# A mixture's first product as seven block products of Strassen's scheme, with its joined weights kept in DRAM

## The chip, the cores and the metric

The kernel runs on one core of one Trainium2 chip. The metric is device time in microseconds (us), the median of several executions. The core has TensorE (PE, matmuls, which write to PSUM), VectorE (DVE), ScalarE (ACT), GpSimd (POOL) and SyncE (SP, which issues nearly all DMAs here). Each engine takes its instructions in the order in which they were recorded.

## The reference

Two parts, one after the other, in float32:

```
attention:  B=4, H=8, S=768, D=64; q and k are assigned to one of 16 clusters;
            scores between different clusters are masked; softmax; times v
x = attention output as [4, 768, 512]
h = (x^T U) V ;  u = x + h^T                    (rank 32, over the 768 positions)
ch = max(u @ w_ch1, 0) @ w_ch2                  (512 -> 2048 -> 512)
out = u + ch
```

The products `u @ w_ch1` and `max(...) @ w_ch2` are what the change works on; the text calls them the first and the second product. The weights arrive as 64-bit words, and the kernel makes float32 of them with a scaling on ACT (`upper`) and three bit operations on DVE (`join`).

## The kernel before, in words

The attention runs over 16 pairs of heads (`i` = 0 to 15, 12 steps of time each). Every function is put into a list with a time (`at(time, fn, ...)`, in units of such steps); the list is sorted by time and then run, so that the table of numbers decides the order of the instructions on every engine, and `keep_order` fixes it. `M0` is the time at which the mixture begins. The order says nothing about durations: an engine waits where its next instruction's operands are not there.

To reach float32 accuracy with the fast matmul type, every operand of the mixture is split into a high part (a cast on ACT) and a low part (a subtraction), and each product takes three matmuls: high times high, high times low, low times high.

The mixture before goes over 8 half batches of 384 rows (`i`) and 16 tiles of 128 hidden columns (`f`). `gemm1(i, f)` makes 12 matmuls (4 tiles of the 512 inputs, three each) with 384 moving columns into one PSUM bank (L629, L630, L631). ACT takes the positive part as `hh` (L634), DVE the low rest as `hl` (L635). `gemm2(i, f)` makes 9 matmuls with 512 columns (3 tiles of rows, three each) into three banks `y` (L645 to L647). `finish(i)` adds `u` (L653) and writes out. `turn_u` transposes `u` for the next half batch and splits it (L618, L620, L621).

The weights lie split in SBUF from their joining to the end, in four groups of 8 pieces of 128x512 (`load_weights`): group 0 is joined during the attention, group 1 towards its end, groups 2 and 3 in the first steps of the mixture. The low parts are subtracted by POOL, four of group 1 by DVE (L208). A piece's joining is L174, L175, L177 with a result in PSUM on the way, or L181, L183, L186 in SBUF alone. POOL otherwise adds up the softmax weights (L515). Work tiles in PSUM (`work`) are 4 banks throughout, `y` another 4.

The order on SP: loads for the attention, raw weights (`rw`), `u` to DRAM and back (`u_scr`), outputs. `rowmax_place` sends the negative row maxima of the scores through a small DMA from ACT's queue (`arena<-mT`), and the second half of each score matmul (L502) waits for it.

## Time and profile before

| what | us |
|---|---|
| median of 3 runs (lowest, highest) | 1023.95 (1021.68, 1024.12) |
| span of the profiled execution, its first to its last instruction | 1023.5 |
| PE busy | 999.9 |
| DVE, ACT, POOL busy | 488.9, 350.6, 361.8 |
| DMA, moved | 87.71 MB |

The profiled execution's own time is known as its span alone; it lies between the runs' lowest and highest. Busy PE time is counted with modelled ends of matmuls that overlap, so that distances between starts are used below where a matmul's price is needed. The mixture's first matmul starts at 468.34 us of the span. A row of the timeline gives start, duration, engine, line, operation, tile written and tiles read, count, and in brackets the idle time ahead of it and what ended it.

### The profile page before, as it was taken

What the parts mean: (1) busy time and instruction counts of PE and PEld (TensorE: products, weight loads), DVE (VectorE), ACT (ScalarE), POOL (GpSimd) and SP (SyncE); (2) the same over time, 40 slices, a digit from 0 to 9 for tenths busy, and PEclk for the clock granted to TensorE, in tenths of its full rate; (3) what the DMA queues carried; (4) which work ended last, traced back from release to release, by engine and by line L of the source; (5) the groups of instructions that cost most, each with busy time, mean ns of one, the idle gap of its engine ahead of it and who ended that gap; (6) DMA issues with size and microseconds to landing.
All of it is one profiled execution on the core that took longest, in us unless ns stands there. A gap on an engine that the chain in (4) does not pass through costs nothing.

```text
span 1023.5 us, 13820 instructions
## 1 busy us (share of the span) xinstructions
PE 999.9 (98%) x5419; PEld 796.3 (78%) x5419; DVE 488.9 (48%) x914; ACT 350.6 (34%) x573; POOL 361.8 (35%) x246
## 2 busy tenths in 40 slices
...
GB/s 164 190 132 128 145 148 104 199 156 156 108 207 139 125 109 180 58 131 107 188 111 63 1 4 59 1 62 1 1 62 1 2 61 1 62 1 1 31 1 31
DMA packets 28675, 87.71 MB, mean 86 GB/s; under 512 B 4874, under 2 KB 9476, under 8 KB 28100
## 3 DMA queue, kind: packets, MB, share of 16 engines
...
q8 instruction: 42, 0.69, 0.3%
...
## 4 chain that ended last, share of the span: by engine, by line
PE 90%; DVE 5%; ACT 1%; issue 1%; DMA 1%; POOL 1%; ACTq 0%; SPq 0%; DVEq 0%; POOLq 0%
PE o_ps L523 12%; PE ps_h L629 9%; PE ps_h L631 9%; PE ps_h L630 9%; PE y L647 9%; PE y L646 9%; PE y L645 9%; PE ps_max L462 7%; PE st L500 6%; PE st L502 6%; DVE m L464 2%; PE ps_sim L352 1%; PE ps_sum L535 1%; PE ps_uT L618 1%; PE ps_oT L556 1%
## 5 line engine op out<-in xcount | busy, mean ns | idle before, releaser
L515 POOL TENSOR_TENSOR T<-T,pr 128x768 f32<-128x768 f32 x120 | 228.1, 1901 | 48.9 <-ACT pr L505 20.5
L635 DVE SCALAR_TENSOR_TENSOR hl<-ps_h,hh 128x384 fp32r<-128x384 f32 x128 | 71.3, 557 | 360.9 <-ACT hh L634 360.9
L464 DVE TENSOR_REDUCE m<-ps_max 128x1 f32<-128x384 f32 x384 | 195.4, 547 | 85.4 <-PE ps_max L462 83.5
L634 ACT ACTIVATE hh<-ps_h 128x384 fp32r<-128x384 f32 x128 | 62.9, 492 | 381.3 <-PE ps_h L631 381.3
L505 ACT ACTIVATE pr<-st 128x768 f32<-128x768 f32 x192 | 154.8, 811 | 81.2 <-PE st L502 63.3
L523 PE MATMUL o_ps<-pr,vt 128*64 128x384 f32 x768 | 133.7, 499 | 0.0
L462 PE MATMUL ps_max<-arena 128*128 128x384 f32 x384 | 125.8, 376 | 7.7 <-ACT sims L355 2.4
L646 PE MATMUL y<-w2l,hh 128*128 128x512 f32 x288 | 113.6, 395 | 0.0
L500 PE MATMUL st<-arena 128*128 128x384 f32 x384 | 106.0, 357 | 1.8 <-ACT pr L505 1.8
L523 PEld LDWEIGHTS o_ps<-pr,vt 128*64 128x64 f32 x768 | 53.2, 139 | 68.0 <-issue 62.8
L462 PEld LDWEIGHTS ps_max<-arena 128*128 128x128 f32 x384 | 70.3, 191 | 44.5 <-issue 17.9
L502 PE MATMUL st<-arena 97*128 97x384 f32 x384 | 100.4, 343 | 2.9 <-DMA arena<-mT 2.7
L500 PEld LDWEIGHTS st<-arena 128*128 128x128 f32 x384 | 66.3, 191 | 17.7 <-issue 9.9
L515 POOL TENSOR_TENSOR T<-pr 128x768 f32<-128x768 f32 x30 | 56.4, 1881 | 60.7 <-ACT pr L505 60.7
L647 PE MATMUL y<-w2h,hl 128*128 128x512 f32 x192 | 76.1, 396 | 0.0
L647 PE MATMUL y<-arena,hl 128*128 128x512 f32 x192 | 76.0, 396 | 0.0
L645 PE MATMUL y<-w2h,hh 128*128 128x512 f32 x192 | 75.1, 391 | 0.0
L645 PE MATMUL y<-arena,hh 128*128 128x512 f32 x192 | 74.8, 390 | 0.0
L502 PEld LDWEIGHTS st<-arena 97*128 97x128 f32 x384 | 71.1, 192 | 3.9 <-issue 2.8
L646 PEld LDWEIGHTS y<-w2l,hh 128*128 128x128 f32 x288 | 54.0, 188 | 9.1
L527 ACT COPY os<-o_ps 128x384 f32<-128x384 f32 x32 | 15.3, 479 | 106.5 <-PE o_ps L523 106.5
L629 PE MATMUL ps_h<-arena,w1h 128*128 128x384 f32 x128 | 44.7, 350 | 0.2 <-DVE arena L621 0.2
...
## 6 DMA issues: line engine op xcount, KB each, us to landing
...
```

What stands on the lines that cost most here:

```text
L462: nc.tensor.matmul(ps[:, 0:HS], x1[:, 0, g // 2, g % 2, t * P:(t + 1) * P], x1[:, 1, h, g % 2, :], start=True, stop=True)
L464: nc.vector.reduce_max(live["m2", i][:, h, u:u + 1], ps[:, 0:HS], axis=AX.X)
L500: nc.tensor.matmul(st[:, j, 0:HS], x1[:, 1, hk, j, ks], x1[:, 0, h, j, :], start=True, stop=False)
L502: nc.tensor.matmul(st[:, j, 0:HS], x2[0:97, 1, hk, j, ks], x2[0:97, 0, h, j, :], start=False, stop=True)
L505: nc.scalar.activation(pr, st[:, :, 0:HS], AF.Exp, scale=SCALE)
L515: eng.tensor_add(T, live["p", i, h, 0] if c == 1 else T, live["p", i, h, c])
L523: nc.tensor.matmul(o_ps[64 * j:64 * j + 64, 0:HS], vv[:, c, j, :], pr[:, j, :], start=(c == 0), stop=(c == NT - 1))
L629: nc.tensor.matmul(ps[:, 0:HS], w1h[:, d, fs], uh[:, d, :], start=(d == 0), stop=False)
L630: nc.tensor.matmul(ps[:, 0:HS], w1h[:, d, fs], ul[:, d, :], start=False, stop=False)
L645: nc.tensor.matmul(y[t], hh[:, ts], w2h[:, f % FG, :], start=(f == 0), stop=False)
L646: nc.tensor.matmul(y[t], hh[:, ts], w2l[:, f % FG, :], start=False, stop=False)
L647: nc.tensor.matmul(y[t], hl[:, ts], w2h[:, f % FG, :], start=False, stop=(f == NF - 1))
```

## The change

The first product of a whole batch is computed by blocks. `u` transposed (512 x 768) is cut into 2 x 2 blocks `b11` to `b22` of 256 inputs by 384 rows; the weights of two tiles of hidden columns (`k` and `k + 8`) into 2 x 2 blocks `a11` to `a22` of 128 columns by 256 inputs. Four sums of the `a` (`s1` to `s4`, L653, POOL) and four of the `b` (`t1` to `t4`, L627, POOL) are made, and seven products of one `a` or `s` with one `b` or `t` (Winograd's form of Strassen's scheme) stand for eight. A product is 6 matmuls of 384 columns (L687 to L689). Where PSUM added up before, seven additions of DVE that read the product in PSUM (L697) and one copy of ACT (L701) now put the results together in SBUF tiles `c0` and `c1`; `hh` and `hl` are then made of two tiles at once, 128x768 (L730, L727), from SBUF.

A group `g` is one batch `b` with one pair `k` of tiles: 4 batches x 8 pairs = 32 groups, each 7 products and 6 `gemm2` of 6 matmuls (L740 to L742). The `gemm2` of a group stand between the products of the next. The work tiles in PSUM are 2 banks from `M0` on, `y` 6.

The joined weights are no longer kept split in SBUF. Each joined half block is written to DRAM (`w_scr`, L211), and for every group its 128x1024 block of the first and of the second weights are read back (`fetch_w`, L644), summed (L653) and split (`split_w` L660 and L662, `split_w2` L669 and L671): high parts on ACT, the low ones of the first weights on POOL in batch 0 and on DVE afterwards, those of the second weights on POOL. 16 of the 32 joinings stand in the attention, from its fourth pair of heads to its twelfth (pace 6.5), 16 in groups 1 to 5 (pace 1.985, where a group is 7). Joining in the mixture works in SBUF alone: L189, L190, L192.

`u` of batch 0 is fetched, turned and split within the last two pairs of heads, that of the next batch in groups `k` = 5 to 7: 8 turns (L620, copies on ACT L622), four sums on POOL (L627), seven splits (ACT L633, DVE L634). The many times of the attention's tables are shifted slightly.

The order at three places. First, DVE while weights are being joined in the mixture (before: half batch 0; `rv`, `xt` belong to the last pair of heads):

```order
L545 TENSOR_SCALAR rv<-ps_sumT 128x12
L547 RECIPROCAL rv<-rv 128x12
L557 TENSOR_TENSOR xt<-ps_oT,rv 128x3x128
L635 SCALAR_TENSOR_TENSOR hl<-ps_h,hh 128x384
L181 TENSOR_SCALAR rw_t<-rw_g 128x512
L186 SCALAR_TENSOR_TENSOR rw_t<-rw,rw_t 128x512
L183 SCALAR_TENSOR_TENSOR rw_t<-rw_g,rw_t 128x512
```

and now, in group 2 (`c_5406` is its `c0`):

```order
L697 TENSOR_TENSOR c_5406<-ps_h,rw_g 128x384
L189 TENSOR_SCALAR rw_b<-rw_g 128x512
L190 SCALAR_TENSOR_TENSOR rw_b<-rw_g,rw_b 128x512
L192 SCALAR_TENSOR_TENSOR rw_t<-rw,rw_b 128x512
L697 TENSOR_TENSOR rw_g<-ps_h,rw_g 128x384
L697 TENSOR_TENSOR rw_t<-ps_h,rw_g 128x384
```

Between two results of PE there was one `hl`; now the three operations of a joining stand between additions that empty PSUM. Of these joinings groups 1 to 5 hold 2, 4, 3, 4 and 3.

Second, DVE at the change of batch, before (`y_5101` is the half batch that ends):

```order
L621 TENSOR_TENSOR ul<-ps_uT,uh 128x384
L635 SCALAR_TENSOR_TENSOR hl<-ps_h,hh 128x384 x2
L653 TENSOR_TENSOR u<-y_5101,u 128x512
L653 TENSOR_TENSOR u<-y_5102,u 128x512
L653 TENSOR_TENSOR u<-y_5103,u 128x512
L635 SCALAR_TENSOR_TENSOR hl<-ps_h,hh 128x384 x11
```

and now, from group 6 into group 7 of batch 0:

```order
L634 TENSOR_TENSOR arena<-turned,arena 128x768
L697 TENSOR_TENSOR c_6142<-ps_h,rw_t 128x384
L727 SCALAR_TENSOR_TENSOR hl<-c_6142,hh 128x768
L634 TENSOR_TENSOR arena<-turned,arena 128x768 x2
L697 TENSOR_TENSOR c_6201<-ps_h,rw_g 128x384
L634 TENSOR_TENSOR arena<-turned,arena 128x768
L697 TENSOR_TENSOR rw_g<-ps_h,rw_g 128x384
L660 TENSOR_TENSOR combos_107<-rw,combos_107 128x768
```

The splitting of the next operand was four short operations per half batch that read PSUM; it is seven of 128x768 per batch that read SBUF alone, put between the additions of one group's length.

Third, PE where the last pair of heads is mixed (`mix_v`: L585 before, L578 now), before:

```order
L647 MATMUL y_5103<-arena,hl 128x512
L585 MATMUL ps_h<-x_5293,v_133 128x512 x3
L629 MATMUL ps_h<-arena 128x384
L630 MATMUL ps_h<-arena 128x384
L631 MATMUL ps_h<-arena 128x384
```

and now, behind group 0's last product:

```order
L687 MATMUL ps_h<-arena,combos_107 128x384
L688 MATMUL ps_h<-arena,combos_107 128x384
L689 MATMUL ps_h<-arena,combos_107 128x384
L578 MATMUL ps_h<-x_5187,v_145 128x512 x3
L687 MATMUL ps_h<-arena,combos_5077 128x384
L688 MATMUL ps_h<-arena,combos_5077 128x384
L689 MATMUL ps_h<-arena,combos_5077 128x384
```

Three `mix_v` had a whole tile step (12 + 9 matmuls) between them and the next three; now there is one product of 6 matmuls.

The diff, cut to what is spoken of:

```
-NG = 4
-FG = NF // NG
+NK = NF // 2
...
+PACE, LATE, EARLY = 6.5, 1.985, 16
...
+    "add_w":    (   0.2,    0.8,    1.4,      2),
+    "split_w":  (  2.12,    2.5,  4.908,    5.3),
+    "relu":     (   4.3,    4.5,    6.2,    6.4),
+    "split_w2": (   3.1,    3.5),
...
+    w_scr = [[dram.tile([P, 1024], F32, name=f"w_scr{k}_{m}") for m in range(2)] for k in range(NK)]
...
+        t = home[0].tile([P, 512], I32, name="rw_t")[0:r, 0:n]
+        b = (work("ps_t").bitcast(I32) if home[0] is raw else home[0].tile([P, 512], I32, name="rw_b"))[0:r, 0:n]
+        nc.vector.tensor_scalar(b, g, 3, None, op0=ALU.logical_shift_left)
+        nc.vector.scalar_tensor_tensor(out=b, in0=g, scalar=-0x80000000, in1=b,
+                                       op0=ALU.bitwise_and, op1=ALU.bitwise_or)
+        nc.vector.scalar_tensor_tensor(out=t, in0=low, scalar=29, in1=b,
+                                       op0=ALU.logical_shift_right, op1=ALU.bitwise_or)
+        return rw, g, t
...
+    blocks = sorted(((k, m) for k in range(NK) for m in range(2)), key=lambda x: (x[0] + x[1], -x[1]))
+
+    def load_weights(s, stage):
+
...
+            nc.sync.dma_start(out=w_scr[k][m][:, cols], in_=parts.pop(("w", s))[2].bitcast(F32))
+            stored.add((k, m, half))
...
-        hi, lo = (x[:, d, :] for x in turned[i % 2])
-        nc.scalar.copy(hi, ps[:, 0:HS])
-        nc.vector.tensor_sub(lo, ps[:, 0:HS], hi)
...
-        ps = work("ps_h")
-        for d in range(ND):
-            nc.tensor.matmul(ps[:, 0:HS], w1h[:, d, fs], uh[:, d, :], start=(d == 0), stop=False)
-            nc.tensor.matmul(ps[:, 0:HS], w1h[:, d, fs], ul[:, d, :], start=False, stop=False)
-            nc.tensor.matmul(ps[:, 0:HS], w1l[:, d, fs], uh[:, d, :], start=False, stop=(d == ND - 1))
...
+    def operand(b, o):
+
+        s = (7 * b + order.index(o)) % 9
+        at = 0 if s == 8 else 2 * XS + 2 * HB * s
+        return [arena[:, at + k * HB:at + (k + 1) * HB].rearrange("p (d q) -> p d q", d=2) for k in range(2)]
+
...
+        pool["w"] = ctx.enter_context(tc.tile_pool(name="ps_m", bufs=2, space=PSUM, side="right", reuse_waits="tile"))
+        pool["y"] = ctx.enter_context(tc.tile_pool(name="ps_y", bufs=6, space=PSUM, reuse_waits="tile"))
+        combos.append(sb.tile([P, 2, 1792], F32R, name="combos1"))
+        live["w2", 0] = sb.tile([P, 2, 2, 512], F32R, name="w2_0")
...
+    def add_u(o):
+
+        i0, i1 = {"t3": ("b22", "b12"), "t1": ("b12", "b11"), "t2": ("b22", "t1"), "t4": ("t2", "b21")}[o]
+        nc.gpsimd.tensor_sub(homes[o], homes[i0], homes[i1])
+
+    def split_u(b, o):
+
+        x = homes[o]
+        hi, lo = (m.rearrange("p d q -> p (d q)") for m in operand(b, o))
+        nc.scalar.copy(hi, x)
+        nc.vector.tensor_sub(lo, x, hi)
...
+    def fetch_w(k, m):
+
+        if m == 0:
+            t = raw.tile([P, 512], I64, name="rw").bitcast(F32)
+        else:
+            t = pool["sb"].tile([P, 1024], F32, name="w2f")
+        live["f", k % NK, m] = t
+        nc.sync.dma_start(out=t, in_=w_scr[k % NK][m])
...
+    def add_w(k, o):
+
+        x, s = live["f", k % NK, 0], sums_w
+        a21, a11, a12, a22 = (x[:, 256 * i:256 * i + 256] for i in range(4))
+        s2, s3, s1, s4 = (s[:, 256 * i:256 * i + 256] for i in range(4))
+        out, op, i0, i1 = {"s1": (s1, ALU.add, a21, a22), "s3": (s3, ALU.subtract, a11, a21),
+                           "s2": (s2, ALU.subtract, s1, a11), "s4": (s4, ALU.subtract, a12, s2)}[o]
+        nc.gpsimd.tensor_tensor(out=out, in0=i0, in1=i1, op=op)
+
+    def split_w(k, part, low):
+
+        x, cols = (live["f", k % NK, 0][:, 256:1024], slice(0, 768)) if part == 0 else (sums_w, slice(768, 1792))
+        hi, lo = (combos[k % 2][:, m, cols] for m in range(2))
+        if low:
+            (nc.gpsimd if k < NK else nc.vector).tensor_sub(lo, x, hi)
+        else:
+            nc.scalar.copy(hi, x)
+
+    def split_w2(k, low):
+
+        x = live["f", k % NK, 1]
+        hi, lo = (live["w2", k % 2][:, m].rearrange("p f n -> p (f n)") for m in range(2))
+        if low:
+            nc.gpsimd.tensor_sub(lo, x, hi)
+        else:
+            nc.scalar.copy(hi, x)
+
+    products = (("a11", "b11"), ("a12", "b21"), ("s2", "t2"), ("s3", "t3"), ("a22", "t4"), ("s1", "t1"), ("s4", "b22"))
+
...
+        b, k = divmod(g, NK)
+        a, o = products[p]
+        c0 = 256 * factors.index(a)
+        ah, al = (combos[k % 2][:, m, c0:c0 + 256].rearrange("p (d f) -> p d f", d=2) for m in range(2))
+        oh, ol = operand(b, o)
+        ps = work("ps_h")[:, 0:HS]
+        for d in range(2):
+            nc.tensor.matmul(ps, ah[:, d], oh[:, d], start=(d == 0), stop=False)
+            nc.tensor.matmul(ps, ah[:, d], ol[:, d], start=False, stop=False)
+            nc.tensor.matmul(ps, al[:, d], oh[:, d], start=False, stop=(d == 1))
+
...
+        if p == 0:
+            live["p1"] = temp("rw_g")
+            nc.scalar.copy(live["p1"], ps)
+        elif p == 1:
+            combine(half(0)[:, 0], ps, live["p1"])
+        elif p == 2:
+            live["u2"] = temp("rw_g")
+            combine(live["u2"], ps, live.pop("p1"))
+        elif p == 3:
+            live["u3"] = temp("rw_t")
+            combine(live["u3"], ps, live["u2"])
+        elif p == 4:
+            combine(half(0)[:, 1], live["u3"], ps, ALU.subtract)
+        elif p == 5:
+            u4 = temp("rw_t")
+            combine(u4, ps, live.pop("u2"))
+            live["u4"] = u4
+            combine(half(1)[:, 1], ps, live.pop("u3"))
+        else:
+            combine(half(1)[:, 0], ps, live.pop("u4"))
+
+    def gemm2(g, j):
+        b, k = divmod(g, NK)
+        if k == 0:
+            live["y", b, j] = pool["y"].tile([P, 512], F32, name=f"y_{j}", tag="y")
+        t, q = divmod(j, HT)
+        y, (hh, hl), w2 = live["y", b, j], live["h", g, t], live["w2", k % 2]
+        ts = slice(q * P, (q + 1) * P)
+        for f in range(2):
+            nc.tensor.matmul(y, hh[:, f, ts], w2[:, 0, f, :], start=(k == 0 and f == 0), stop=False)
+            nc.tensor.matmul(y, hh[:, f, ts], w2[:, 1, f, :], start=False, stop=False)
+            nc.tensor.matmul(y, hl[:, f, ts], w2[:, 0, f, :], start=False, stop=(k == NK - 1 and f == 1))
...
+    for g in range(ng):
+        b, k = divmod(g, NK)
+        m = M0 + 7 * g
+        own = mlp[("first", "second")[g]] if g < 2 else None
+        relus, w2s = (own[7:11], own[11:13]) if own else (mlp["relu"], mlp["split_w2"])
+        for p in range(7):
+            at(m + (own[p] if own else p), product, g, p)
+        for k4, step in enumerate(relus):
+            at(m + step, relu, g, k4 // 2, k4 % 2 == 1)
+        for low, step in enumerate(w2s):
+            at(m + step, split_w2, g, low == 1)
+        if g + 1 < ng:
+            weights_of(g + 1, m)
+            at(m + mlp["fetch_w"][0], fetch_w, g + 1, 1)
+        if g + 2 < ng:
+            at(m + mlp["fetch_w"][1], fetch_w, g + 2, 0)
+        for j in range(6):
+            m2 = m + (own[13 + j] if own else 7 + mlp["gemm2"][0] + mlp["gemm2"][1] * j if g + 1 < ng else 7 + 0.1 * j)
+            at(m2, gemm2, g, j)
+            if k == NK - 1:
+                at(m2 + 0.3 if g + 1 < ng else m2 + 0.05, finish, b, j)
...
+            elif k == NK - 2:
+                for h in range(2):
+                    for d in range(ND):
+                        at(m + mlp["turn_u"][0] + mlp["turn_u"][1] * (ND * h + d), turn_u, b + 1, h, d)
+                splits(m, b + 1, mlp["split"])
...
+    w1 = bits["w1"].reshape(2, 2, P, 2, NK, P).transpose(4, 0, 3, 2, 1, 5)
+    w1 = np.stack([w1[:, d, f] for f, d in ((1, 0), (0, 0), (0, 1), (1, 1))], axis=2)
+    w2 = bits["w2"].reshape(2, NK, P, DM).transpose(1, 2, 0, 3)
+    weights = np.stack([w1.reshape(NK, P, 1024), w2.reshape(NK, P, 1024)], axis=1)
```

286 lines of the change are left out of this document (145 added, 141 removed).

## The prediction

> **What bounds the kernel now.** I read the page's busy lines first, then the busy times by stretches, then PE's timeline, then the durations of single lines.
>
> ```profile
> span 1023.5 us, 13820 instructions
> PE 999.9 (98%) x5419; PEld 796.3 (78%) x5419; DVE 488.9 (48%) x914; ACT 350.6 (34%) x573; POOL 361.8 (35%) x246
> PE 90%; DVE 5%; ACT 1%; issue 1%; DMA 1%; POOL 1%; ACTq 0%; SPq 0%; DVEq 0%; POOLq 0%
> 100.00:400.00 300.00, 297.34 (x1798) 202.34 (x1799) 226.08 (x447) 169.96 (x247) 239.82 (x130) 1.00 0.55 146
> 583.00:651.40 68.40, 68.40 (x350) 61.84 (x350) 12.93 (x23) 9.79 (x20) 0.00 (x0) 1.00 0.07 24
> ```
>
> The last two rows are stretches of the attention and of the mixture (length, then busy PE, weight loads, DVE, ACT, POOL, granted clock, DMA). PE is the bound in both. In the mixture nothing else is near: of 68.4 us DVE works 12.9, ACT 9.8, POOL none. Whatever PE need not do there comes off the end, as long as the idle engines do what replaces it in time. So there are two questions: what does PE save, and where does it begin to wait.
>
> ```profile
> 702.48 0.33 PE L629 MATMUL ps_h<-uh,arena 128*128 128x384 f32 x1
> 704.41 0.34 PE L631 MATMUL ps_h<-uh,arena 128*128 128x384 f32 x1
> 704.58 0.39 PE L645 MATMUL y<-arena,hh 128*128 128x512 f32 x1
> 706.66 0.33 PE L629 MATMUL ps_h<-uh,arena 128*128 128x384 f32 x1
> ```
>
> Distances between starts are the price: 12 matmuls of the first product take 704.58 - 702.48 = 2.10 us, 0.175 each; 9 of the second 2.08, 0.231 each.
>
> **What PE saves.** The first product goes from 1536 matmuls (8 x 16 x 12) to 1344 (32 x 7 x 6), of the same 384 columns and with one weight load each; the second product's 1152 and the transposes stay. 192 x 0.175 = **33.6 us**. A group then takes PE 42 x 0.175 + 36 x 0.231 = 15.67 us. Left alone this gives 1023.5 - 33.6 = 989.9.
>
> **What the other engines get.** The nearest rows:
>
> ```profile
> L621 DVE TENSOR_TENSOR ul<-ps_uT,uh x16: 542/557/558, 524.2 to 947.0; 128x384 fp32r<-128x384 f32 x16
> L515 DVE TENSOR_TENSOR T<-T,pr x8: 945/954/2021, 58.5 to 466.9; 128x768 f32<-128x768 f32 x8
> L183 DVE SCALAR_TENSOR_TENSOR rw_t<-rw_g,rw_t x16: 691/692/1670, 470.9 to 536.1; 128x512 int32<-128x512 int32 x16
> L186 DVE SCALAR_TENSOR_TENSOR rw_t<-rw,rw_t x16: 679/687/694, 470.1 to 535.4; 128x512 int32<-128x512 int32 x16
> L181 DVE TENSOR_SCALAR rw_t<-rw_g x16: 408/418/759, 469.6 to 533.6; 128x512 int32<-128x512 int32 x16
> L515 POOL TENSOR_TENSOR T<-T,pr x120: 1804/1846/2493, 40.6 to 468.0; 128x768 f32<-128x768 f32 x120
> L208 POOL TENSOR_TENSOR w2l<-rw_t,arena x4: 1283/1294/1298, 488.8 to 502.2; 128x512 fp32r<-128x512 f32 x4
> L505 ACT ACTIVATE pr<-st x192: 789/812/832, 35.2 to 462.7; 128x768 f32<-128x768 f32 x192
> ```
>
> (Minimum, median, maximum in ns.) A DVE addition that reads a product in PSUM: 0.56 us. DVE on two SBUF operands: 0.95 for 768, 0.69 for 512, so on that line 1.21 for 1024. POOL: 1.85 for 768, 1.29 for 512, so 2.40 for 1024 and 0.74 for 256. A joining on DVE: 0.42 + 0.69 + 0.69 = 1.80.
>
> A late group (batches 1 to 3): DVE 7 x 0.56 + 2 x 0.95 (`hl`) + 0.95 + 1.21 (low weights) = 8.0 us; POOL 4 x 0.74 + 2.40 = 5.4; ACT, at 0.8 to 1.1 for each of six operations, under 6. All fit into 15.67. Two PSUM banks mean that a product's bank must be read before the product after next. Between them lies mostly a product and two `gemm2` steps (1.05 + 2 x 1.39 = 3.8 us), behind the first and the seventh product 2.4. The tightest is the seventh's: it ends at 15.7 of the group (16.0 with 0.3 us until DVE sees it). DVE does `hl` of the first half from 12.7, then the two additions of the sixth and the 1024 low weights until 16.0, and has read the seventh at 16.6; the bank is wanted at 18.1. I take **0** for the late groups. If a POOL subtraction of 2.40 got in front of the low weights, the cover of 1.5 would be gone and 0.9 lost, 22 us over 24 groups.
>
> **Groups 1 to 5, where weights are still joined.** Here DVE and POOL meet:
>
> ```profile
> 500.75 0.69 DVE L183 SCALAR_TENSOR_TENSOR rw_t<-rw_g,rw_t 128x512 int32<-128x512 int32 x1
> 513.50 0.68 DVE L186 SCALAR_TENSOR_TENSOR rw_t<-rw,rw_t 128x512 int32<-128x512 int32 x1
> 514.22 1.67 DVE L183 SCALAR_TENSOR_TENSOR rw_t<-rw_g,rw_t 128x512 int32<-128x512 int32 x1
> 513.58 1.76 POOL L208 TENSOR_TENSOR w1l<-rw_t,w1h 128x512 fp32r<-128x512 f32 x1 [2.43 <-ACT w1h L207]
> ```
>
> The same DVE line takes 0.69 us alone and 1.67 when it starts within a POOL subtraction (513.58 to 515.34), ending 0.55 behind it; POOL's, which began while L186 ran, takes 1.76 instead of 1.29. They exclude one another. Before, one such pair stood in each 4.2 us of PE's work, and nothing waited. Now POOL has 4 x 0.74 + 1.85 + 2 x 2.40 = 9.6 us a group, DVE on two SBUF operands 1.9 (`hl`) and 1.38 a joining. Groups 1 to 5 with 16 joinings: 5 x 11.5 + 16 x 1.38 = 79.6 us that exclude one another, against 5 x 15.67 = 78.4 of PE. DVE alone has 5 x 5.8 + 16 x 1.80 = 57.8, POOL 48; neither is the bound by itself, the pair is. Lower bound 0, since some low weights are made 4 us ahead of need. Upper bound: each of the 32 joining operations on two SBUF operands and the ten `hl` waits 0.98 (1.67 - 0.69), 41 us, less DVE's free 78.4 - 57.8 = 20.6: 20.5. What queues behind them is the addition that empties a bank, and behind that PE. I take **7**, nearer the sum than the upper end.
>
> The Trainium skill (SBUF — State Buffer, section "Who interferes with whom") says that such a port pair is an exclusive lock, held for a whole instruction, and that `tensor_scalar` can take it too. By it the joining's first operation counts as well, 16 x 0.42 = 6.7 us more. Here L181's median of 418 against its maximum of 759 leaves that open; its sum would be 86.3 us, 8 over PE's.
>
> **Three changes of batch.** 7 `split_u` on DVE (6.65 us), 4 sums on POOL (7.4), 15 operations on ACT. They stand in about one group's length, between additions. The work that excludes itself there: 6.65 + 7.4 + 5.4 + 1.9 + 2.2 = 23.5 in 15.67; 7.9 over, of which the next group, 9.5 of 15.67, takes up 6. DVE itself has 14.6. Bounds 0 and 7.9 each; I take 2.5, **7.5** for three.
>
> **The start of the mixture.**
>
> ```profile
> 500.45 0.87 PE L585 MATMUL ps_h<-x,v 96*128 96x512 f32 x3
> 501.36 1.88 DVE L586 TENSOR_TENSOR xt<-ps_h,xt 128x512 f32<-128x512 f32 x3
> 505.32 0.87 PE L585 MATMUL ps_h<-x,v 96*128 96x512 f32 x3
> ```
>
> Six `mix_v` now pass through two banks with one product between them: PE has 6 x 0.23 + 1.05 = 2.4 us, DVE 2 x 1.88 and an `hl` of 0.95, 4.7. PE waits 2.3, and some more for the banks that the attention gives back: **3** (0 to 6).
>
> **The attention.**
>
> ```profile
> 437.16 0.62 PE L500 MATMUL st<-arena 128*128 128x384 f32 x2 [1.41 <-ACT pr L505]
> 439.75 0.98 PE L502 MATMUL st<-arena 97*128 97x384 f32 x2 [1.97 <-DMA arena<-mT]
> 440.65 6.77 PE L523 MATMUL o_ps<-pr,vt 128*64 128x384 f32 x24
> 453.05 4.09 PE L523 MATMUL o_ps<-pr,vt 128*64 128x384 f32 x24
> 440.65:447.40 6.75, 6.75 (x26) 2.52 (x25) 2.18 (x4) 0.81 (x1) 1.88 (x1) 0.60 0.74 268
> ```
>
> Before the last scores PE stands for 3.4 us, and the next 24 matmuls run at a granted clock of 0.60 and take 2.7 longer than the same 24 later: 6.1 us. Around that place stood group 1's joinings, low weights and 512 KB loads; now the joinings end two pairs of heads earlier, and batch 0's eight copies, seven splits and four POOL sums come near instead. Eight more joinings in between add to DVE's 75% of the stretch 100 to 400, and 16 stores come into SP's order. I take half of the stall back, **-3**, bounds -6 and +6.
>
> The sum: 1023.5 - 33.6 + 7 + 7.5 + 3 - 3 = 1004.4. The median of the runs before is 0.45 above the span, so the forecast for the median is **1005**.
>
> **The rivals.** *All covered* (0.24): POOL's and DVE's pieces slip past one another in their slack; only the start costs. What speaks for it is the stretch of the late groups, for it and against it the sum of 79.6 against 78.4. 989.9 + 3 - 3 = 990.
>
> *The pair of DVE and POOL becomes the bound* (0.13): each operation on two SBUF operands waits for one of POOL's in groups 1 to 5 and at the changes of batch, as L183 did at 514.22. 20.5 and 3 x 7.9 in place of 7 and 7.5: 1034, slower than before. It decides from the point where these waits exceed 33.6 us in all. For it: alternation is what the rows show whenever both have work; against it: half of POOL's work in a group can run where DVE has none of this kind.
>
> *The clock drops* (0.06): in each of the eight places where I have PE wait (five groups, three changes), the following matmuls lose 2.7 us as at 440.65: 1004.4 + 21.6 = 1026. Against it: there PE had stood for 3.4 us, almost in one piece, and my waits are 1 to 2.5. The Trainium skill (TensorE: Matmul & The Clock Gate, section "What's actually happening") gives about 3.4 us of idleness for the gate; by that rule this rival would not occur, and the trace's one drop agrees with it.
>
> *The late groups lose their cover* (0.05): 1004.4 + 22 = 1026. Against it: POOL's next work, the sums of the weights, overwrites what those low weights are made of and so cannot stand in front of them.
>
> *PE does not get faster by the matmuls left out* (under 0.01), since each carries a weight load of 0.188 that goes with it; it would give 1038.
>
> **How the numbers follow.** The forecast as summed has 0.50, with its own range 996 to 1013. For 8 in 10 I go down to the rival without waits and up to where half of the pair's extra loss (1034 - 1004 = 30) has come about: **989 to 1020**. About 0.3% (3 us) is what a measurement can tell here, so faster means below 1020.9, slower above 1027. Faster: 0.50 + 0.24 + 0.08 (milder forms of the last three) = 0.82; same 0.07; slower 0.11, nearly all the pair's.
>
> **What would show it.** Each product of 6 matmuls starts 1.05 us behind the last one's start where nothing is between; a late group takes 15.7 us, and in windows of late groups PE is busy throughout. POOL's busy sum should rise from 362 to about 557 us (28 subtractions of L208, 39 us, go; 24 of 768, 40 of 1024 and 128 of 256 come). PE's waits should name L697's additions, in groups 1 to 5 and around the changes of batch, and no others of weight; DVE's L190 should show a maximum far above its minimum of 0.69, and none in batches without POOL beside it. Wrong would be: waits on the weights' DMAs, waits in the late groups, a granted clock below 1 in the mixture, or a stall of the old size before the last scores.

## The result, and the profile after

The median rose from 1024.03 to **1056.45 us** (1055.12 to 1058.02), a ratio of 1.0319 with a 95% interval of 1.0304 to 1.0334: slower, where 1005 and a range of 989 to 1020 had been forecast. The profiled execution took 1058.02, 1.8 of it outside its span. Its page and three stretches (length, busy PE, weight loads, DVE, ACT, POOL, granted clock, DMA):

```profile
span 1056.2 us, 14186 instructions
PE 986.9 (93%) x5227; PEld 766.5 (73%) x5227; DVE 703.6 (67%) x1114; ACT 446.4 (42%) x633; POOL 590.3 (56%) x410
PE 62%; DVE 18%; DMA 7%; issue 4%; ACT 3%; POOL 3%; SPq 1%; ACTq 0%; DVEq 0%; POOLq 0%
100.00:400.00 300.00, 276.04 (x1607) 184.39 (x1607) 218.66 (x423) 153.74 (x223) 204.17 (x109) 0.98 0.60 162
518.60:615.20 96.60, 86.36 (x399) 73.78 (x400) 79.95 (x94) 32.93 (x45) 53.44 (x33) 0.96 0.64 210
671.80:734.40 62.60, 62.60 (x313) 56.17 (x312) 33.60 (x45) 19.56 (x25) 24.24 (x22) 1.00 0.34 121
```

PE's share of the chain of waits is 62% where it was 90%. In the attention (first stretch) PE stands for 24 us of 300, before it was 3. In groups 1 to 5 of the mixture (second) DVE works for 80 of 97 us. In four late groups (third) PE has no idle time. The first product's first matmuls, of the mixture and of three late groups:

```profile
503.39 0.45 PE L687 MATMUL ps_h<-arena,combos 128*128 128x384 f32 x1
656.09 0.33 PE L687 MATMUL ps_h<-arena,combos 128*128 128x384 f32 x1
671.76 0.33 PE L687 MATMUL ps_h<-arena,combos 128*128 128x384 f32 x1
687.41 0.33 PE L687 MATMUL ps_h<-arena,combos 128*128 128x384 f32 x1
```

A late group takes 15.66 us, as forecast. But the mixture starts at 503.4 instead of 468.3. The largest single piece, in SP's, ACT's and PE's timelines:

```profile
183.91 1.78 SPq L581 DMA_DIRECT2D u_scr<-xt  x1
185.75 0.43 SPq L171 DMA_DIRECT2D rw<-in_w  x1
197.28 0.66 ACT L179 ACTIVATE rw_g<-rw 128x512 f32<-128x512 f32 x1 [10.19 <-DMA rw<-in_w]
199.57 1.55 PE L516 MATMUL o_ps<-pr,vt 128*64 128x384 f32 x4 [5.99 <-ACT pr L498]
```

A raw load is issued right behind a batch's store of 1536 KB. ACT's half of the joining stands for 10.2 us in front of the exponentials, and PE for 6.0. The next five pairs of heads take 28 to 31 us each, before 25 to 28. Behind its waits PE also runs slower:

```profile
222.49 1.33 PE L528 MATMUL ps_sum<-T,sel 128*32 128x384 f32 x8 [2.06 <-DVE rw_t L192]
198.00:206.00 8.00, 6.43 (x21) 5.15 (x22) 4.08 (x8) 4.57 (x7) 2.85 (x2) 0.57 0.62 159
222.00:226.00 4.00, 3.51 (x15) 2.44 (x16) 3.12 (x7) 0.98 (x2) 2.05 (x2) 0.59 0.66 173
642.00:650.00 8.00, 6.40 (x19) 5.81 (x20) 6.71 (x8) 3.22 (x4) 7.92 (x6) 0.57 0.01 2
sum 36.00, PE 31.55 PEld 24.80 DVE 25.08 ACT 14.30 POOL 23.31; mean PE 4.51 PEld 3.54 DVE 3.58 ACT 2.04 POOL 3.33
```

From 100 us on there are seven such drops (four in the attention, three in the mixture); the last row sums their windows, in which PE is busy for 31.6 us at a mean clock of 0.57 to 0.59: about 13 us lost, by this estimate. The kernel before has two drops behind its first 50 us, in these windows:

```profile
90.00:96.00 6.00, 5.24 (x24) 3.48 (x24) 5.15 (x9) 2.32 (x3) 5.15 (x3) 0.72 0.70 149
438.00:446.00 8.00, 6.25 (x20) 2.63 (x22) 4.80 (x6) 1.80 (x3) 4.37 (x3) 0.58 0.73 253
```

In the same way they lose about 4 us, so that by this estimate some 9 of the 32 us that the kernel lost are the clock's. Times in the next section are medians of the fast runs; one run of 1887 us (e14) and one of 4235 us (e17) are left out.

### The profile page after: what moved, and what is told of

The parts are those of the page before. It is cut to its first block, busy times and chain, and to the rows that moved or that the text cites. A ratio compares the mean times of both kernels' runs of the same rounds, so it can differ in the third digit from the quotient of the medians.

```text
span 1056.2 us, 14186 instructions
## 1 busy us (share of the span) xinstructions
PE 986.9 (93%) x5227; PEld 766.5 (73%) x5227; DVE 703.6 (67%) x1114; ACT 446.4 (42%) x633; POOL 590.3 (56%) x410
## 4 chain that ended last, share of the span: by engine, by line
PE 62%; DVE 18%; DMA 7%; issue 4%; ACT 3%; POOL 3%; SPq 1%; ACTq 0%; DVEq 0%; POOLq 0%
PE o_ps L516 9%; PE y L741 6%; PE y L742 6%; PE y L740 6%; PE ps_h L687 6%; PE ps_h L688 6%; PE ps_h L689 6%; PE ps_max L455 5%; DMA rw<-in_w 4%; PE st L493 4%; PE st L495 4%; DVE m L457 3%; DVE arena L634 2%; DVE rw_t L192 2%; DVE hl L727 2%
## 5 line engine op out<-in xcount | busy, mean ns | idle before, releaser
L457 DVE TENSOR_REDUCE m<-ps_max 128x1 f32<-128x384 f32 x384 | 195.3, 548 | 108.9 <-PE ps_max L455 107.3
L687 PE MATMUL ps_h<-arena,combos 128*128 128x384 f32 x448 | 154.2, 344 | 15.6 <-DVE c L697 15.0
L730 ACT ACTIVATE hh<-c 128x768 fp32r<-128x768 f32 x64 | 54.2, 846 | 243.6 <-DVE c L697 243.6
L742 PE MATMUL y<-w,hl 128*128 128x512 f32 x384 | 153.0, 399 | 1.8 <-DVE hl L727 1.7
L741 PE MATMUL y<-w,hh 128*128 128x512 f32 x384 | 153.9, 401 | 0.0
L740 PE MATMUL y<-w,hh 128*128 128x512 f32 x384 | 152.5, 397 | 0.0
L688 PE MATMUL ps_h<-arena,combos 128*128 128x384 f32 x448 | 151.5, 338 | 0.0
L689 PE MATMUL ps_h<-arena,combos 128*128 128x384 f32 x448 | 151.2, 338 | 0.0
L653 POOL TENSOR_TENSOR sums_w<-rw 128x256 f32<-128x256 f32 x64 | 52.6, 842 | 156.8 <-DVE combos L660 126.2
L669 POOL TENSOR_TENSOR w<-w2f,w 128x1024 fp32r<-128x1024 f32 x32 | 78.3, 2447 | 77.3 <-ACT w L671 74.1
L727 DVE SCALAR_TENSOR_TENSOR hl<-c,hh 128x768 fp32r<-128x768 f32 x64 | 76.3, 1193 | 52.4 <-ACT hh L730 52.4
L687 PEld LDWEIGHTS ps_h<-arena,combos 128*128 128x128 f32 x448 | 84.9, 190 | 32.5 <-DVE c L697 18.6
L508 POOL TENSOR_TENSOR T<-pr 128x768 f32<-128x768 f32 x30 | 57.0, 1899 | 87.0 <-ACT pr L498 86.8
L688 PEld LDWEIGHTS ps_h<-arena,combos 128*128 128x128 f32 x448 | 85.0, 190 | 7.6
```

What stands on the lines that cost most here:

```text
L457: nc.vector.reduce_max(live["m2", i][:, h, u:u + 1], ps[:, 0:HS], axis=AX.X)
L508: eng.tensor_add(T, live["p", i, h, 0] if c == 1 else T, live["p", i, h, c])
L687: nc.tensor.matmul(ps, ah[:, d], oh[:, d], start=(d == 0), stop=False)
L688: nc.tensor.matmul(ps, ah[:, d], ol[:, d], start=False, stop=False)
L689: nc.tensor.matmul(ps, al[:, d], oh[:, d], start=False, stop=(d == 1))
L740: nc.tensor.matmul(y, hh[:, f, ts], w2[:, 0, f, :], start=(k == 0 and f == 0), stop=False)
```

## The experiments

Each edit is shown against the changed kernel; one that adds lines shifts the line numbers behind it (L687 is L688 in e9). The columns: where the mixture's first product starts, how long groups 1 to 5 take, both from the starts of the first product in each profile, and the median. One group is 15.66 us; groups 1 and 2 hold 3 us of the last pair's mixing as well.

| kernel | first product at | groups 1 to 5 | median | ratio to before |
|---|---|---|---|---|
| before | 468.3 | | 1024.03 | 1 |
| changed | 503.4 | 96.7 | 1056.45 | 1.0319 |
| e1 no joining | 474.2 | 81.3 | 1011.42 | 0.9883 |
| e2 no late joining | 503.5 | 81.3 | 1041.26 | 1.0170 |
| e3 no store | 505.5 | 95.4 | 1052.72 | 1.0285 |
| e4 store later | 503.5 | 96.8 | 1057.27 | 1.0327 |
| e5 load earlier | 509.5 | 96.3 | 1058.17 | 1.0334 |
| e6 no DVE passes | 488.8 | 81.3 | 1026.98 | 1.0038 |
| e7 in place | 547.9 | 97.4 | 1101.91 | 1.0772 |
| e8 pace 9.6 | 520.5 | 97.5 | 1072.54 | 1.0490 |
| e9 old places | 484.3 | 97.3 | 1040.68 | 1.0168 |
| e10 two passes | 509.8 | 91.2 | 1054.52 | 1.0283 |
| e11 e9 and e10 | 504.3 | 89.3 | 1050.28 | 1.0256 |
| e12 remainders on DVE | 505.5 | 92.5 | 1053.26 | 1.0277 |
| e13 no new operands | 505.2 | 96.8 | 1045.15 | 1.0212 |
| e14 e9 and e12 | 490.0 | 94.9 | 1038.59 | 1.0138 |
| e15 e14, two passes late | 488.5 | 84.3 | 1030.06 | 1.0053 |
| e16 half a pair later | 498.7 | 97.9 | 1054.44 | 1.0300 |
| e17 all together | 482.7 | 86.8 | 1024.07 | 1.0005 |
| e18 and buffers | 480.1 | 88.6 | 1019.74 | 0.9956 |

The 95% intervals of the ratios are widest in e9, e10, e12 and e13, where they reach 4 to 6 us to either side. Smaller differences are read from the starts in the profiles.

### What the joinings cost: e1, e2

e1 joins nothing (e2, with `range(EARLY)` in the same line, the first 16 halves), and 1024 floats a partition of the q/k input are read instead:

```
-    for s in range(4 * NK):
+    for s in range(0):
...
-        nc.sync.dma_start(out=t, in_=w_scr[k % NK][m])
+        nc.sync.dma_start(out=t, in_=qk[k % NK // 2, k % 2 * 2 + m].rearrange("p s q -> p (s q)")[:, 0:1024])
```

> The changed kernel with all 32 joinings of weights left out, with their raw loads, halves on ACT, three DVE passes and stores; the first product and its sums read 1024 finite numbers a partition of the q/k input in their place, by transfers of the same size at the same places, so the output is not the reference's. It gives the whole price of the joinings as this kernel places them. Theory A (the joinings, through SP's ordered queue or through their own work, are what went wrong): the first product of the mixture starts at 468 us or earlier (503.4 in the changed kernel, 468.3 before), groups 1 to 5 of the mixture fall from the measured 96.7 us to about 78.4, and the whole comes to about 1056 - 35 - 18 = 1003 us. Theory B (the attention's loss comes from its shifted table of times, which stands whether or not anything is joined): the first product still starts near 500 us and the whole comes to about 1036 us. In both the three changes of batch keep their losses of some 14 us, because nothing is joined there.

> The changed kernel with the 16 joinings of the mixture's first batch left out and the 16 of the attention kept; blocks that were not joined are read from the q/k input, so the output is not the reference's. Theory A: the first product stays at about 503 us, groups 1 to 5 come down from 96.7 to about 78.4 us, the whole to about 1038 us. If the losses of groups 1 to 5 come from the work that every group of a first batch does on POOL and DVE beside each other (its sums, splits and remainders) and not from the joinings, the five groups stay above 90 us and the whole above 1048 us.

Without any joining the mixture starts at 474.2 and the whole takes 1011.42: the joinings cost 45.0 us, of which the attention's 16 have 29.8 and the mixture's 16 have 15.2. As stretches, first the same pair of heads in the changed kernel and without joinings, then the attention up to the mixture's first product in both, then group 0 and groups 1 to 5 without joinings:

```profile
230.00:259.30 29.30, 27.28 (x160) 18.23 (x159) 20.73 (x42) 15.84 (x24) 22.83 (x13) 1.00 0.65 176
214.50:240.70 26.20, 26.12 (x161) 18.20 (x159) 18.21 (x35) 14.96 (x22) 22.39 (x12) 1.00 0.54 136
45.30:503.39 458.09, 422.75 (x2453) 279.42 (x2452) 328.30 (x614) 235.95 (x344) 320.45 (x173) 0.98 0.53 142
45.30:474.22 428.92, 412.96 (x2453) 276.70 (x2453) 298.28 (x566) 228.57 (x328) 320.87 (x173) 0.99 0.47 122
474.22:489.39 15.17, 13.57 (x70) 9.38 (x69) 8.13 (x16) 6.44 (x9) 10.05 (x9) 1.00 0.12 36
489.39:570.70 81.31, 80.92 (x399) 72.01 (x400) 33.21 (x49) 23.68 (x30) 49.99 (x35) 1.00 0.31 110
```

DVE has 2.5 us more to do in the pair, is busy for 71% of it and so is not its bound, and the pair is 3.1 us longer. With the joinings PE is idle for 35.3 us of the attention instead of 16.0, and the same 2453 matmuls keep it busy for 9.8 us more; in groups 1 to 5 it is idle for 10.2 us instead of 0.4 and busy for 5.4 more. The clock has a part in that longer busy time.

Theory A stands, though the whole ends 8 us above its 1003. What is left of the attention's loss without joinings (theory B) is 474.2 - 468.3 = 5.9 us. Of it about 2.4 us are no loss: 12 transposes (1.5 us) and 8 sums of the last pair (0.9 us) stood behind the mixture's first product before and now stand ahead of it. The kernel before has 16 joinings of its own in the attention; what they cost there, no run shows. Even so 1011 is far from 990: most of the rest is in the changes of batch (e13).

By the table of times groups 1 to 5 hold 2, 3, 4, 3 and 4 of the mixture's joinings, and not 2, 4, 3, 4 and 3 as was said above. In the changed kernel they take 19.5, 17.7, 21.3, 16.6 and 21.7 us, without joinings 17.3, 17.1 and three times 15.7: a group with three joinings loses about 1 us, one with four about 6 (group 1, which also mixes, 2). No run has a pace of three to a group.

### Which part of a joining: e3, e4, e5, e6

The times of e4 (stores later) and e5 (loads earlier), then the store that e3 and e6 leave out and the passes that e6 leaves out as well; both read the q/k input as e1 does:

```
-    "w":    (36.161, 38.329, 40.954,  43.05),
-    "late": ( 9.201,   10.9,   11.5,   12.3),
+    "w":    (36.161, 38.329, 40.954,   46.3),
+    "late": ( 9.201,   10.9,   11.5,   14.3),
...
+    "w":    (  29.5, 38.329, 40.954,  43.05),
+    "late": (   7.9,   10.9,   11.5,   12.3),
...
-            nc.sync.dma_start(out=w_scr[k][m][:, cols], in_=parts.pop(("w", s))[2].bitcast(F32))
+            parts.pop(("w", s))
...
-            parts["w", s] = join(*parts["w", s])
+            pass
```

> The changed kernel with all 32 joinings kept (raw load, half on ACT, three DVE passes) but their stores to DRAM left out, so that nothing on SP's queue waits for a joined tile; the sums and products read the q/k input, so the output is not the reference's. Theory A1 (the store waits in SP's ordered queue for the join, and the loads and copies of rows behind it come late): the first product falls from 503.4 to about 475 us, groups 1 to 5 to about 84 us, the whole to about 1015 us. Theory A2 (the joining's own work on DVE and ACT and its loads): the first product stays above 495 us, the whole above 1045 us.

> The changed kernel complete, with each store of a joined tile 3.25 slots (some 7 us) later in the attention's order and 2 turns later in the mixture's; nothing is left out. Theory A1 (SP stands at the store, and what is behind it is late): the store finds its tile ready, SP's wait for the joined tiles falls from some 77 us in 100 to 400 us to under 15, the first product moves to about 480 us and the whole to about 1025 us. Theory A2 (the work itself): under 8 us of gain, the whole above 1048 us.

> The changed kernel complete; the raw load of every joining stands 6.66 slots (some 15 us) earlier in SP's order in the attention and 1.3 turns earlier in the mixture, where it is as early as its two buffers let it be. The stores have been ruled out (leaving them out gave 4 us, placing them later nothing), and the joinings of the attention cost 29.8 us (1041.3 less 1011.4), those of the mixture 15.2 (1056.5 less 1041.3). Theory A (ACT stands for the load that was issued too late, 10.2 us in one place at 187 to 197 us, and the exponentials behind it are late): the pair of heads after 190 us comes down from 39.8 to about 28 us, the attention gains 10 to 15 us, groups 1 to 5 some 5 to 10, the whole comes to about 1037 us. Theory B (the three DVE passes hold the row maxima up, and PE with them): at most 10 us from the one stall in the attention, none in the pairs behind it (29 to 31 us each, as before), none in groups 1 to 5, the whole at about 1046 us or above.

> The changed kernel with the three DVE passes of every joining and its store left out; the raw load and the half on ACT stay. The sums and products read the q/k input, so the output is not the reference's. Against the kernel without any joining (1011.4 us) this has the loads and ACT's halves, against the one without the stores (1052.7) it lacks the DVE passes and the PSUM buffer that they take. Theory A (the loads, and ACT that waits for them): the whole stays above 1035 us, the pairs of heads at 230 to 350 us stay at 29 to 31 us. Theory B (the DVE passes): the pairs at 230 to 350 us fall to 26 to 28 us, groups 1 to 5 to about 82 us, the whole to about 1015 to 1022 us.

My first theory, that SP stands at the store and makes the loads behind it late, falls: SP did stand there for 56.6 us of 100 to 400 (not the 77 of the expectation), but leaving the stores out gives 3.7 us, and placing them later cuts that wait to 5.4 us and gains nothing. What counts are the DVE passes, 1052.72 - 1026.98 = 25.7 us (14 of them in groups 1 to 5), and the loads with ACT's halves, 1026.98 - 1011.42 = 15.6, all in the attention. By the starts of the first product, e3's passes cost 505.5 - 488.8 = 16.7 us in the attention; its profiled run was its slowest.

Without the passes e6 also needs no PSUM buffer (`ps_t`) for the joining. The third pass (L192) reads that buffer last, and in the changed kernel PE's waits name this pass for 6.6 us of 100 to 400; the two longest entries:

```profile
PE ps_max L455 <- DVE rw_t L192: 2.4, 3, 1.0
PE ps_sum L528 <- DVE rw_t L192: 2.1, 1, 2.1
```

The waits of `ps_max` on a row maximum (L457) are 1.8 us there, and 1.3 without joinings. So 25.7 us are the price of the passes together with their buffer.

Loading earlier does not help, though ACT's wait of 10.2 us goes: the longer pair falls from 39.8 to 34.0, the next rises from 29.3 to 35.0. The load now meets the copies of rows, for which PE waits longest in 100 to 400:

```profile
PE ps_max L455 <- DMA arena<-arena: 9.0, 3, 4.0
```

### How DVE's passes cost: e7, e8

e7 writes the first two passes into the third's own SBUF tile, e8 changes the pace:

```
-        b = (work("ps_t").bitcast(I32) if home[0] is raw else home[0].tile([P, 512], I32, name="rw_b"))[0:r, 0:n]
+        b = t
...
-PACE, LATE, EARLY = 6.5, 1.985, 16
+PACE, LATE, EARLY = 9.6, 1.985, 16
```

> The changed kernel complete, with the first two passes of a joining written into the third's own SBUF tile, so that the joining takes none of the attention's four PSUM buffers. Theory B1 (what PE waits for is the PSUM buffer, which lies in one rotation with the row maxima and comes free only after the third pass): PE's waits for the joined tile go, the pairs at 230 to 350 us come down by 1 to 3 us each, the whole to about 1045 us. Theory B2 (what counts is the time of the passes on DVE): the passes become longer, because in SBUF they stand beside POOL's additions (0.92 us the first and 1.00 the second on average in the mixture's SBUF form, against 0.68 and 0.70 in PSUM), and the whole stays or comes to 1056 to 1065 us.

> The changed kernel complete, with the 16 joinings of the attention 9.6 slots apart in place of 6.5, so that they reach over the whole attention (slots 36 to 187) and there are 1.25 of them in a pair of heads in place of 1.85. Theory C (a joining costs nothing until a pair of heads holds more of them than its slack takes; the kernel before held one in a pair and lost nothing by them): the pairs at 190 to 350 us fall to about 27 us, the later ones rise by less than 1 each, the whole comes to about 1040 us. Theory D (every joining costs its own 1.9 us wherever it stands): the loss is only spread, the first product stays within 5 us of 503.4 and the whole within 5 us of 1056.

The second pass in the attention (100 to 400 us) in the changed kernel, then all three in e7, as groups of lines, and what PE waits for longest there:

```profile
L190 DVE SCALAR_TENSOR_TENSOR ps_t<-rw_g,ps_t 128x512 int32<-128x512 int32 (+1 forms) x17 | 11.7, 688 | 0.6
L190 DVE SCALAR_TENSOR_TENSOR rw_t<-rw_g,rw_t 128x512 int32<-128x512 int32 (+1 forms) x15 | 26.9, 1792 | 0.5
L192 DVE SCALAR_TENSOR_TENSOR rw_t<-rw,rw_t 128x512 int32<-128x512 int32 (+1 forms) x15 | 22.1, 1474 | 0.5
L189 DVE TENSOR_SCALAR rw_t<-rw_g 128x512 int32<-128x512 int32 (+1 forms) x15 | 17.8, 1189 | 0.0
PE ps_max L455 <- DVE m L457: 17.6, 9, 4.1
```

In SBUF, beside POOL's additions, the second pass takes 1.79 us instead of 0.69, and the whole 45 us more; B2 was right in kind and five times too small. The waits for the third pass go, as B1 had it, and waits for row maxima come in their place. So a microsecond of DVE at these places is paid more than whole: three passes of 16 joinings became some 39 us longer (1.19 + 1.79 + 1.47 less 3 x 0.68, times 16). What the buffer alone costs, e7 does not tell, because it changes both. e8 is against both of its theories: fewer joinings in a pair, and 16 us slower. The number in a pair is not what decides; the places are different ones in each.

### Where a joining stands: e9, e16

e9; in e16 the four times of `"w"` are 41.66, 44.22, 48.54 and 49.30. In both, and in all kernels with the old places, the fetch of group 1's first weights also moves behind the joinings (fourth time of `"open"`, from -40 to -3.5):

```
-    "w":    (36.161, 38.329, 40.954,  43.05),
+    "w":    ( 35.66,  38.22,  42.54,  43.30),
+    "end":  (-26.11, -21.73,  -20.5, -18.35),
...
-            at(stages["w"][stage] + PACE * s if s < EARLY else M0 + stages["late"][stage] + LATE * (s - EARLY),
-               load_weights, s, stage)
+            at(stages["w"][stage] + NS * s if s < 8 else
+               M0 + stages["end"][stage] + 2.04 * (s - 8) if s < EARLY else
+               M0 + stages["late"][stage] + LATE * (s - EARLY), load_weights, s, stage)
```

> The changed kernel complete, with the 16 joinings of the attention put where the kernel before has its first 16: eight 12 slots apart from slot 36 (one in a pair of heads, its load 2.6 slots and more ahead of ACT's half), eight 2.04 slots apart in the last 26 slots, where most row maxima are done; the transfer of the second weights' pair is moved behind them, because it would hold one of the two raw buffers. Measured so far: of the attention's 29.8 us, 14.6 come from the loads and ACT's halves and 16.7 from the three DVE passes (2.04 us a joining, 32.7 us of DVE in all). Theory E (a DVE pass costs only where it stands in front of row maxima that PE waits for, and a load only where it meets a batch's store of 1536 KB; the old places have neither): the pairs at 190 to 350 us fall to 26 to 28 us, the first product to about 478 us, the whole to about 1031 us. Theory D (each joining costs its 1.9 us wherever it stands): the first product stays near 503 us and the whole within 8 us of 1056.

> The changed kernel complete, with the old places of the joinings in the attention but the first eight all 6 slots (half a pair of heads) later; still one in a pair, 12 slots apart. Against the old places (first product at 484.3 us, pairs of heads from the sixth on 28.5, 26.3, 31.0, 27.7, 28.6, 26.2 us): if the phase against the row maxima and the copies of rows decides, these pairs become 1 to 3 us longer each and the first product comes to 490 to 497 us; if the number in a pair decides, the first product stays within 3 us of 484.

With the old places the mixture starts 19 us earlier, which is 6 us short of theory E; the eight in the last 26 slots cost nothing (pairs of 30.8, 27.7, 27.7 us against 30.8, 27.0, 28.3 without any joining). The first eight still cost about 10 us (484.3 against 474.2). The same eight half a pair later lose 14.4 of the 19 again. First products, and SP's waits in 100 to 350 us, of e9 and then of e16:

```profile
484.28 0.44 PE L688 MATMUL ps_h<-arena,combos 128*128 128x384 f32 x1
SPq L212 <- DVE rw_t L193: 10.0, 8, 1.7
...
498.67 0.44 PE L688 MATMUL ps_h<-arena,combos 128*128 128x384 f32 x1
SPq L212 <- DVE rw_t L193: 63.3, 5, 15.7
```

The place decides: e16 differs from e9 in nothing else. The two reasons that theory E gives for it are not separated, and what in the place counts is not one thing: in e16 SP waits up to 15.7 us at a store with copies of rows behind it, in the changed kernel such waits cost next to nothing. I did not separate that from DVE's passes in e16.

### DVE and POOL in the mixture's first batch: e10, e11, e12, e14, e15

The two passes (`z` is the zero with the sign, made on ACT), in e10 and e11 for all joinings, in e15 for the mixture's, where `z` gets a bias of -0.0; then the remainders on DVE (e12, e14, e15):

```
+        nc.scalar.mul(z.bitcast(F32), high, 0.0)
...
-        nc.vector.tensor_scalar(b, g, 3, None, op0=ALU.logical_shift_left)
-        nc.vector.scalar_tensor_tensor(out=b, in0=g, scalar=-0x80000000, in1=b,
-                                       op0=ALU.bitwise_and, op1=ALU.bitwise_or)
-        nc.vector.scalar_tensor_tensor(out=t, in0=low, scalar=29, in1=b,
-                                       op0=ALU.logical_shift_right, op1=ALU.bitwise_or)
+        nc.vector.scalar_tensor_tensor(out=b, in0=low, scalar=29, in1=z,
+                                       op0=ALU.logical_shift_right, op1=ALU.bitwise_or)
+        nc.vector.scalar_tensor_tensor(out=t, in0=g, scalar=3, in1=b,
+                                       op0=ALU.logical_shift_left, op1=ALU.bitwise_or)
...
-            (nc.gpsimd if k < NK else nc.vector).tensor_sub(lo, x, hi)
+            nc.vector.tensor_sub(lo, x, hi)
```

> The changed kernel complete, with the joining done in two DVE passes in place of three: ACT makes the sign as a zero of the number's sign (the upper word times 0.0, one more ACT pass of some 0.66 us), DVE joins it to the lower word's three bits and then to the shifted upper word. If the DVE passes are what costs, a third of their price goes: of 16.7 us in the attention 5.6, of 14.3 us in the mixture 4.8, the whole to about 1046 us. If ACT's work is what costs as much (its halves and the loads cost 14.6 us in the attention), the attention loses on ACT what it gains on DVE and the whole stays within 4 us of 1056, with the gain in groups 1 to 5 alone.

> The changed kernel complete, with the old places of the joinings and the joining in two DVE passes together. By theory E and the price of the passes: first product at about 476 us, groups 1 to 5 at about 92 us, the whole at about 1024 us, no difference from the kernel before. By theory D: the whole at about 1046 us, as with the two passes alone.

> The changed kernel complete, with the remainders of the first weights in the first batch made on DVE as in the later batches, in place of POOL (12 subtractions in groups 1 to 5 that took POOL 27.4 us). Theory F (DVE and POOL shut each other out on SBUF, which makes the passes of 0.68 us in PSUM 0.93 to 1.16 us in SBUF): the three passes come down from 3.08 to about 2.4 us, which repays part of the 15 us that the subtractions add on DVE, and groups 1 to 5 come to 95 to 100 us, the whole within 4 us of 1056. Theory G (no such exclusion, DVE is simply full: 80.0 of 96.6 us): the passes keep their 3.08 us and the five groups grow by about 12 us, the whole to about 1068 us.

> The changed kernel complete, with the old places of the attention's joinings (1040.7 us alone) and the remainders of the first weights on DVE in the first batch (1053.3 alone, 3.2 under the changed kernel). The two lie in different stages, so the gains add: about 1037 us. If the first product's start decides how the mixture's first groups meet their weights, the second gain may be lost: 1041 us.

> The changed kernel complete, with both changes of the last one and, in the mixture alone, the joining in two DVE passes, where ACT makes the sign as the upper word times zero plus a minus zero (times zero alone gave no usable sign). Groups 1 to 5 of the mixture fell from 96.7 to 91.2 us by two passes alone and to 92.6 by the remainders on DVE alone; if DVE's fill is the limit there, the two add to about 87 us and the whole comes to about 1031 us; if something else holds the groups by then (the loads, ACT), they stay at 91 us and the whole at 1036.

In e10, e11 and e15 the weights so joined lose their sign, so these leave out the sign; the work is that of two passes. The groups of lines in groups 1 to 5 of the changed kernel, with what PE waits for longest there, and then of e12, which takes 23 us of subtractions from POOL and gives DVE 13:

```profile
PE ps_h L687 <- DVE c L697: 8.6, 4, 3.4
L727 DVE SCALAR_TENSOR_TENSOR hl<-c,hh 128x768 fp32r<-128x768 f32 x10 | 15.5, 1554 | 4.6 <-ACT hh L730 4.6
L190 DVE SCALAR_TENSOR_TENSOR rw_b<-rw_g,rw_b 128x512 int32<-128x512 int32 x15 | 14.8, 989 | 0.5
L189 DVE TENSOR_SCALAR rw_b<-rw_g 128x512 int32<-128x512 int32 x15 | 14.0, 932 | 1.9 <-ACT rw_g L179 1.7
...
L190 DVE SCALAR_TENSOR_TENSOR rw_b<-rw_g,rw_b 128x512 int32<-128x512 int32 x15 | 12.0, 803 | 0.5
L727 DVE SCALAR_TENSOR_TENSOR hl<-c,hh 128x768 fp32r<-128x768 f32 x10 | 10.4, 1037 | 4.6 <-ACT hh L730 4.6
L189 DVE TENSOR_SCALAR rw_b<-rw_g 128x512 int32<-128x512 int32 x15 | 8.5, 564 | 1.9 <-ACT rw_g L179 1.9
```

DVE gets work and is done sooner (77.8 us of 92.5, in the changed kernel 80.0 of 96.6), because its own operations shorten: theory F, with a larger gain than it forecast. The Trainium skill (SBUF — State Buffer, section "Who interferes with whom") says that DVE and GpSimd exclude one another where DVE reads two operands from SBUF and that `tensor_scalar` can take the shared pair too. The rows agree: L189 has one SBUF operand and goes from 0.56 to 0.93 with POOL's work.

Two passes alone bring the groups from 96.7 to 91.2, as expected; in the attention the gain is lost. That ACT's further pass takes it, as the expectation's second reading has it, is argued only: PE's waits that name the last DVE pass rise as well, from 6.6 to 9.5 us. e11 missed its expectation: its last pair of heads takes 46.0 us, where eight joinings hold the two `rw_t` tiles from ACT's pass to the store. Its trace shows it: four times ACT waits for a store from `rw_t`, 20.7 us in all, and PE 18.2 us for the exponentials behind. e14 keeps part of its second gain, since the first weights' remainders now stand on DVE in the last pairs (31.9 and 29.1 us). With two passes late and the remainders on DVE, groups 1 to 5 come to 84.3 us: 12 of the 15 are back. The cause is shown to be the time of DVE's operations, POOL's part in it included. DVE is not full (80.0 of 96.6 us): the additions (L697) that empty PSUM stand behind them, and PE waits for these.

### The changes of batch: e13

```
-                splits(m, b + 1, mlp["split"])
-        oh, ol = operand(b, o)
+        oh, ol = operand(0, o)
```

> The changed kernel with the making of new operands at the three changes of batch left out (the additions on POOL, the copies on ACT, the subtractions on DVE); the later batches multiply with the first batch's operands, so the output is not the reference's. The transposes and their copies stay. The third and fourth batches' changes (groups of 19.0, 18.3 and 16.4 us where 15.66 is a group's own time) should keep the 3.3 us of the transposes in the first and lose 2.65 and 0.7 in the others if DVE, which is busy for 16.5 of 18.3 us in the second, is what costs there: three changes give 10 to 13 us, the whole comes to about 1045 us. If it is the transfers or the finishing of the old batch's rows, which stay, the groups keep 18.3 us and the whole stays within 3 us of 1056.

The last group of a batch and the first of the next, as starts in e13 (765.06 to 780.71 to 796.38), and the former as a stretch without joinings (e1), with DVE's splits in it:

```profile
765.06 0.33 PE L687 MATMUL ps_h<-arena,combos 128*128 128x384 f32 x1
780.71 0.33 PE L687 MATMUL ps_h<-arena,combos 128*128 128x384 f32 x1
796.38 0.33 PE L687 MATMUL ps_h<-arena,combos 128*128 128x384 f32 x1
...
722.90:741.20 18.30, 16.75 (x79) 13.70 (x77) 16.47 (x18) 9.20 (x12) 12.78 (x8) 1.00 0.07 30
L634 DVE TENSOR_TENSOR arena<-turned,arena 128x768 fp32r<-128x768 f32 x7 | 10.0, 1441 | 0.0
```

Both groups take 15.66 without the new operands, 18.3 and 16.4 with them. By the starts of the groups the three changes give 12.6 us, 5.9 in the first and 3.4 and 3.3 in the others; the medians give 11.3, but with an interval of some 5 us. DVE is busy for 16.5 us in the former group, more than a group has, and PE's waits around it (720 to 760 us in e1) name DVE's operations alone. That it is DVE, and not POOL's or ACT's share of the work left out, rests on this.

### Taking it back: e17, e18

e17 is e15 with the first eight stores at 51.40, another sign (`z` is ACT's sign function times two, and an exclusive or takes its exponent bit out again), and:

```
-    "split":    (   5.2,    5.8,  5.676,    6.4,    6.7,    7.1,    7.7,    8.7,    9.7, 10.559,   11.7),
+    "split":    (   5.2,    5.8,  5.676,    6.4,    6.7,    7.1,    7.7,    8.7,   10.4,   13.6,     16),
...
+            (nc.gpsimd if k < 1 or k % NK == 1 and k > 1 else nc.vector).tensor_sub(lo, x, hi)
```

e18 against e17:

```
-    "w":    ( 35.66,  38.22,  42.54,  51.40),
-    "late": ( 9.201,   10.9,   11.5,   12.3),
+    "w":    ( 35.66,  38.22,  42.54,  48.80),
+    "late": (   8.2,   10.9,   11.5,   12.3),
...
+        rw = home[0].tile([P, 512], I64, name="rw", bufs=2 if home[0] is raw else 3)[0:step * len(srcs), 0:n]
```

> The changed kernel complete, with what the experiments point to: the old places of the attention's joinings with the first eight stores put 8.1 slots later, where SP and the transfers are idle; in the mixture the joining in two DVE passes with the sign made on ACT as the sign function times two (its bit is taken out again by an exclusive or against an upper word scaled by 2 to the -96); the remainders of the first weights on DVE except for the first group and the first group of each later batch; and at each change of batch the last three operands split later, the last in the next batch's first group. From the 1030 us that the places, the remainders and the two passes gave together: the changes of batch give back 5 to 8 of the 11.3 us if DVE's fill in the last group of a batch is their cause, the stores and the remainders 0 to 5 us in the attention, the second sign pass on ACT costs 0 to 3. Together 1018 to 1025 us, with 1021 the likeliest; if the later splits stall the first group of the next batch as much as they relieve the last one, 1028 us.

> The changed kernel complete, as the last one, with the first eight stores of joined tiles at 48.8 slots in place of 51.4 (so that none stands right behind a batch's store of 1536 KB on SP's queue), and with three buffers for the raw weights in the mixture in place of two, each load one turn earlier. If the waits for raw loads (14.6 us of ACT) are what the groups 4 and 6 (18.0 and 18.7 us) and 5 are left with, the five groups from 86.8 us come to about 83; the sixth pair of heads from 30.4 to about 27 us. Together some 5 to 7 us: 1018 us, the ratio at 0.994. If DVE's fill and the transfers' share (0.70 in this stretch) hold them, nothing changes but the order of the waits: 1022 to 1025 us.

e17 computes the whole reference and is level with the kernel before (ratio 1.0005, 0.9989 to 1.0021); a change of batch loses 1.9 us where it lost 3.4. e18 is **0.4% faster** than the kernel before: 1019.74, ratio 0.9956 (0.9940 to 0.9973); little, but clear of the interval, and of that of e17. ACT's waits for raw loads in groups 1 to 5 of e17 and e18, then e18's page, and its group 1:

```profile
ACT rw_g L180 <- DMA rw<-in_w: 14.6, 10, 2.6
...
ACT rw_g L180 <- DMA rw<-in_w: 1.9, 2, 1.0
span 1018.0 us, 14199 instructions
493.00:496.00 3.00, 2.10 (x6) 0.83 (x6) 2.93 (x6) 0.84 (x1) 2.75 (x4) 1.00 0.00 0
496.00:499.00 3.00, 2.80 (x9) 1.89 (x9) 1.94 (x3) 1.21 (x2) 0.08 (x1) 0.56 0.00 0
499.00:502.00 3.00, 3.00 (x8) 2.32 (x9) 1.29 (x2) 0.00 (x0) 0.00 (x0) 0.50 0.33 132
```

The sixth pair came to 27.4 us as expected. The five groups did not come to 83 but to 88.6: the waits for loads went, but group 1 took 20.0 instead of 17.3 at a granted clock of 0.5, and the fourth and sixth group (which the expectation calls 4 and 6, counting from one; 17.9 and 18.0) kept most of their loss.

## Why the prediction was wrong

**What PE saves: right.** Late groups take 15.66 us against 15.67, and have no idle time: the 33.6 us are there. So was "a late group 0".

**The attention: the step that failed.** "I take half of the stall back, -3, bounds -6 and +6"; measured +35.1. It priced eight more joinings by their share of a DVE that was 75% busy, and the stores by their place on SP. Without joinings the attention is 5.9 longer, at the upper bound, and 2.4 of that is work moved ahead of the mixture. The 16 joinings add 29.2 (e1), of which half comes from raw loads and ACT's halves (e6), which the step did not mention, and the rest from DVE passes, with their PSUM buffer, that stand before what PE waits for. The same matmuls also keep PE busy for 9.8 us more, in part at a lower granted clock, which the step did not price. The kernel before had one joining in a pair and eight in the last pairs; the step took that for slack of the engine. At these old places the 16 cost about 10 us here (e9 against e1), half a pair later 14 more (e16): it was the place.

**Groups 1 to 5: mechanism right, size off.** 7 against 15.4 measured, within its 0 to 20.5. DVE and POOL do exclude one another there, and L189 belongs to the pair, which the sum of 79.6 left out. Of the 15.4, some 10 are idle time of PE and 5.4 matmuls that take longer, at a mean clock of 0.96, which the term did not hold.

**Changes of batch: size off.** 7.5 against 12.6 (e13). "DVE itself has 14.6" was low: it has 16.5, above a group's 15.66, because its seven splits, beside POOL, take 1.44 us each in place of 0.95.

**The start: nearly right.** 3 against 2.0: in e1 PE is idle for 1.6 us of group 0 and 0.4 of the five behind it. Attention, groups, changes and start put right give 1004.4 + 38.1 + 8.4 + 5.1 - 1.0 = 1055.0 of the span's 1056.2. As 2.4 us of the attention's came over from the mixture, some 3.6 us of the mixture are what I cannot place.

**The rivals.** The pair of DVE and POOL as a bound (1034) came about with half of its extra loss (13.5 of 30 us), and only in the mixture. The clock was set aside because the waits would be 1 to 2.5 us; seven drops came, one behind a wait of 2.06 us, and they are in the prices above. The Trainium skill (TensorE: Matmul & The Clock Gate, section "What's actually happening") gives about 3.4 us of idleness for the gate; here the measurement differs, and e18 shows 0.50 behind 0.9 us of idle PE in pieces. That the kernel before has one drop, which agrees with the rule, was misread: the drop at 91 us, the first of its two windows above, stands behind these waits:

```profile
88.46 0.27 PE L488 MATMUL ps_mT<-ident,m 128*12 128x128 f32 x1 [0.59 <-DVE rw_t L177]
91.04 0.97 PE L502 MATMUL st<-arena 97*128 97x384 f32 x2 [0.76 <-DMA arena<-mT]
```

As signs of error I had named waits on the weights' DMAs and a clock below 1 in the mixture. The clock was there; ACT and POOL waited for the weights (27.3 us on `in_w` and 9.1 on `w_scr` in 503 to 660), PE itself did not.
